# Moving the sum of phi(K) and the weight sums from GpSimd to VectorE, with relu on ScalarE and a fifth plain pair, in a two-layer linear-attention kernel

## The chip, the cores and the metric

The kernel runs on one core of a Trainium2 chip. The metric is the device time of one execution in microseconds (us); lower is better. A time is given as the median of several executions with the lowest and highest beside it.

The engines are written as the profile writes them: PE is the matmul engine, PEld its weight loads (they overlap PE), DVE is VectorE, ACT is ScalarE, POOL is GpSimd, SP is the engine whose queue issues DMAs. In the views `ps` is PSUM, which the matmuls write, and `arena` is the kernel's SBUF. L757 is line 757 of the kernel's source. The change removes and adds lines, so the same place has slightly different numbers before and after: L606 before is L605 after, L757 is L756, L676 is L675, L610 and L619 are L609 and L618, L929 is L927, L1125 is L1126.

## The reference, cut to what matters

Two identical layers follow each other. Each has a linear attention and a gated feed-forward part. S is 2048 tokens, D is 1024, and there are 32 heads of 32.

```python
def _A_ref(x, wqkv, wo):                      # x is already layer-normalised
    qkv = (x @ wqkv).reshape(B, S, 3, H, Dh) ...
    phi = lambda t: jnp.where(t > 0, t + 1, jnp.exp(t)) + 1e-6
    pq, pk = phi(q), phi(k)
    kv  = jnp.einsum("bhsd,bhse->bhde", pk, v)
    z   = jnp.einsum("bhsd->bhd", pk)         # the sum of phi(K) over all tokens
    num = jnp.einsum("bhqd,bhde->bhqe", pq, kv)
    den = jnp.einsum("bhqd,bhd->bhq", pq, z)[..., None] + 1e-6
    ...                                       # (num / den) @ wo

x = x + _A_ref(_layernorm(x), A_wqkv, A_wo)
x = x + _B_ref(_layernorm(x), B_w_gate, B_w_up, B_w_down)
# ... and both lines once more: the second layer, with the same weights
```

Only the K and Q projections, phi, and z are touched by the change.

## The kernel before

The kernel projects K and Q first. For this document that stretch is called the K/Q stage; the stage that forms K^T V starts when it ends. Tokens are handled in tiles of 128, two tiles are a pair, and there are eight pairs.

A pair can be projected in two ways. A *plain* pair takes 64 matmuls of 128x512 (K and Q, two tiles, two column halves, eight contraction steps each). A *quad* is a Strassen–Winograd product with seven block products of four matmuls, 28 for K or Q of one pair, so 56 for both. A quad needs sums of blocks of the weights ("weight sums") and of the normalised x, which are fp16. In layer one the weight sums don't exist yet and layer norms have only begun, so the kernel starts with four plain pairs; the weight sums are formed meanwhile, kept in DRAM, and loaded in layer two, where every pair is a quad.

```python
    NHOLD = 2
    NPL1 = 8
    LNX = (3, 5, 6)
    RLB = (7, 4)
```

`NPL1 = 8` is eight tiles, that is four plain pairs. `RLB` names the PSUM banks whose quad outputs get the relu form of phi, in layer one only.

phi of a 128x512 block has two forms. Both begin with an exponential by ScalarE and a `min(e, 1) + 1e-6` by VectorE. Then either VectorE reads the product from PSUM once more (`scalar_tensor_tensor`), or ScalarE writes `relu` of it to SBUF and VectorE adds two SBUF tiles (`tensor_tensor`).

```python
        def e_min(ev, er):
            P.add("dve", lambda e: e.tensor_scalar(out=ev, in0=ev, scalar1=1.0, scalar2=PHI0, op0=ALU.min, op1=ALU.add), rd=er, wr=er)

        def phi_exp(bank):
            ev, er = e_next()
            P.add("act", lambda e: e.activation(ev, psb(bank), AF.Exp), prd=[bank], wr=er)
            return ev, er

        rl = {"on": False, "n": 0}

        def phi_relu(bank):
            r = rl["n"] % 4
            rl["n"] += 1
            rv, rr = vh(O_XN[r // 2] + r % 2 * 1024, 512), R(O_XN[r // 2] + r % 2 * 1024, 1024)
            P.add("act", lambda e: e.activation(rv, psb(bank), AF.Relu), prd=[bank], wr=rr)
            return rv, rr

        def phi_out(bank, ev, er, dst_ap, dst_rng, rl_=None):
            e_min(ev, er)
            if rl_:
                rv, rr = rl_
                tt(dst_ap, rv, ev, ALU.add, rr + er, dst_rng)
                return
            P.add("dve", lambda e: e.scalar_tensor_tensor(out=dst_ap, in0=psb(bank), scalar=PHI1, in1=ev, op0=ALU.add, op1=ALU.max),
                  prd=[bank], rd=er, wr=dst_rng)

        def phi_evac(bank, dst_ap, dst_rng):
            ee = phi_exp(bank)
            phi_out(bank, *ee, dst_ap, dst_rng, phi_relu(bank) if rl["on"] else None)
```

The weight sums are subtractions of 128x2048 blocks, on whichever engine the caller names, cut into `parts` instructions:

```python
        def tw_make(n, eng, parts):
            b11, b12, b21, b22 = [w_blk(n, kb, h) for kb in range(2) for h in range(2)]
            t1, t2, t3, t4 = [tw_blk(n, c) for c in (1, 2, 3, 4)]
            step = 4 // parts
            ops = []
            for o, a, b in ((t1, b12, b11), (t2, b22, t1), (t4, b21, t2), (t3, b22, b12)):
                for k in range(0, 4, step):
                    def one(o=o, a=a, b=b, k=k):
                        P.add(eng, lambda e: e.tensor_tensor(out=o[0][:, k:k + step], in0=a[0][:, k:k + step], in1=b[0][:, k:k + step], op=ALU.subtract),
                              rd=rsub(a[1], k, step) + rsub(b[1], k, step), wr=rsub(o[1], k, step))
                    ops.append(one)
            return ops
```

Every finished half block of phi(K) is added on GpSimd to an fp32 accumulator; this is the sum over tokens:

```python
            def dst_of(kind, i, h):
                if kind == "k":
                    return pk[:, h, i, :], r_pk(i, h)
                return x_res[:, i, h * 512:(h + 1) * 512], r_x(i, h * 512, (h + 1) * 512)

            def z_add(i, h):
                za, pa = zacc[:, h * 512:(h + 1) * 512], pk[:, h, i, :]
                rz_ = R(O_ZACC + h * 2048, 2048)
                if h not in z_on:
                    z_on.add(h)
                    P.add("pool", lambda e: e.tensor_copy(za, pa), rd=r_pk(i, h), wr=rz_)
                else:
                    P.add("pool", lambda e: e.tensor_tensor(out=za, in0=za, in1=pa, op=ALU.add),
                          rd=r_pk(i, h) + rz_, wr=rz_)

            def proj(kind, i, h):
                t, v, c0, base = WSRC[kind]
                bank = B_KQ[kq_i[0] % len(B_KQ)]
                kq_i[0] += 1

                def fn(e):
                    return [e.matmul(psb(bank), xnT[:, k, i * 128:(i + 1) * 128], t[:, k, h * 512:(h + 1) * 512],
                                     start=(k == 0), stop=(k == KT - 1)) for k in range(KT)]
                P.add("pe", fn, rd=r_xT(i * 128, (i + 1) * 128) + r_w(base, h * 512, (h + 1) * 512), pwr=[bank])

                def ev():
                    phi_evac(bank, *dst_of(kind, i, h))
                    if kind == "k":
                        z_add(i, h)
                return ev
```

The quad gives four phi outputs, two of them through ScalarE's copy `u` and VectorE's `t1`; the two direct ones may use relu:

```python
                def ex(self, bank):
                    self.e = getattr(self, "e", {})
                    self.e[bank] = phi_exp(bank) + ((phi_relu(bank),) if rl["on"] and bank in RLB else (None,))

                def out(self, bank, i, h):
                    ev, er, r = self.e[bank]
                    phi_out(bank, ev, er, *dst_of(self.kind, i, h), r)
                    if self.kind == "k":
                        z_add(i, h)
        # ... cut ...
                def t1(self, j):
                    u, ru = self.u2 if j == 2 else self.u3
                    k = j - 2
                    P.add("dve", lambda e: e.scalar_tensor_tensor(out=t1sb[k], in0=psb(self.Y), scalar=PHI1, in1=u, op0=ALU.add, op1=ALU.add),
                          prd=[self.Y], rd=ru, wr=R(O_T1[k], 1024))
        # ... cut ...
                def out1(self, j, i, h):
                    k = j - 2
                    ev, er = self.e1[j]
                    d, rd_ = dst_of(self.kind, i, h)
                    e_min(ev, er)
                    tt(d, t1sb[k], ev, ALU.max, R(O_T1[k], 1024) + er, rd_)
                    if self.kind == "k":
                        z_add(i, h)
```

The plain part of layer one. The weight sums for K are four VectorE instructions, those for Q sixteen GpSimd instructions:

```python
            NPL = NPL1 if first else 0
            rl["on"] = first
            twk = []
            if first:
                twk = tw_make("k", "dve", 1)
                twq = tw_make("q", "pool", 4)
            seq = [("k", i) for i in range(NHOLD)] if NPL else []
            for i in range(NHOLD, NPL):
                seq += [("q", i - NHOLD), ("k", i)]
            seq += [("q", i) for i in range(max(NPL - NHOLD, 0), NPL if NPL < NST else 0)]
            npack = [0]
            for kind, i in seq:
                for h in range(2):
                    ev = proj(kind, tok[i], h)
                    ev()
                    if kind == "k":
                        lnstep(i, h)
                    elif twq and i >= 1:
                        for _ in range(2):
                            if len(twq) > 4:
                                twq.pop(0)()
                if kind == "q" and i >= 1 and len(twk) > 1:
                    twk.pop(0)()
```

At the end the accumulator is cast by ScalarE and reduced over partitions by a matmul with ones:

```python
            def z_final():
                for h in range(2):
                    P.add("pe", (lambda h: lambda e: e.matmul(psb(B_Z[h]), ones, zab[:, h * 512:(h + 1) * 512], start=True, stop=True))(h),
                          rd=R(O_ONES, 256) + R(O_A[1] + h * 1024, 1024), pwr=[B_Z[h]])
                    P.add("dve", (lambda h: lambda e: e.tensor_copy(zb[:, h * 512:(h + 1) * 512], psb(B_Z[h])))(h),
                          prd=[B_Z[h]], wr=R(O_ZB + h * 1024, 1024))
        # ... cut ...
            P.add("act", lambda e: e.copy(zab, zacc), rd=R(O_ZACC, D * 4), wr=R(O_A[1], D * 2))
```

## Time and profile before

The time before is 1489.12 us, the median of 3 runs (1489.07 to 1490.49). The profiled execution has a span of 1487.0 us.

The first fence is the page of the kernel before: busy time of each engine with its share of the span and its instructions, then the chain of work that ended last, by engine.

```profile
PE 1451.5 (98%) x7512; PEld 720.7 (48%) x7574; DVE 1182.1 (79%) x2218; ACT 595.3 (40%) x1201; POOL 234.0 (16%) x256
...
PE 69%; DVE 18%; DMA 7%; issue 3%; SPq 1%; ACT 1%; POOL 1%; DVEq 0%; ACTq 0%
...
```

PE is busy for 98% of the span, but in the chain DVE has 18%. A chain is followed back from the last instruction to whatever released each step, so for these 18% the end of the kernel hung on VectorE. It doesn't say in which stage; the next view does.

The table by stretches gives the busy time and instruction count of each engine in the K/Q stage of layer one (36 to 125 us) and of layer two (771 to 866 us). Columns after the window are its length, then busy us of PE, PEld, DVE, ACT and POOL, the granted clock, the DMA share and GB/s.

```profile
core 0: us, PE busy (x) PEld busy (x) DVE busy (x) ACT busy (x) POOL busy (x), PEclk, DMA share, GB/s
...
36.00:60.00 24.00, 22.52 (x108) 10.22 (x109) 23.41 (x37) 12.48 (x23) 21.71 (x21) 1.00 0.12 23
60.00:76.00 16.00, 11.42 (x52) 5.02 (x52) 15.41 (x35) 9.94 (x19) 11.02 (x13) 1.00 0.75 150
76.00:125.00 49.00, 43.88 (x183) 19.09 (x187) 47.01 (x92) 28.70 (x51) 24.60 (x24) 0.90 0.65 168
771.00:866.00 95.00, 88.56 (x391) 37.03 (x396) 92.02 (x184) 56.86 (x98) 38.94 (x38) 1.00 0.39 112
```

VectorE is busy for 23.41 of 24.00 us, 15.41 of 16.00, and 92.02 of 95.00. PE has gaps in every one of these windows. GpSimd is nearly full in the first (21.71 of 24.00), and after the switch to quads the granted clock is only 0.90.

The list of waits of PE between 60 and 125 us (engine and line, what it waited for, total us, times, longest):

```profile
engine line waited for: us in total, times, longest us
PE ps L907 <- DVE arena L757: 6.5, 1, 6.5
PE ps L907 <- DVE arena L676: 2.4, 1, 2.4
...
```

The timeline of PE over the same switch (start, length, what ran, and in brackets the idle time before it with its releaser):

```profile
...
71.00 1.03 PE L907 MATMUL ps<-arena 128*128 128x512 bf16 x4
78.52 4.81 PE L907 MATMUL ps<-arena 128*128 128x512 f16 x12 [6.49 <-DVE arena L757]
85.77 38.97 PE L907 MATMUL ps<-arena 128*128 128x512 f16 x169 [2.44 <-DVE arena L676]
124.58 1.67 PE L1125 MATMUL ps<-arena 128*128 128x512 bf16 x7
```

PE waits 6.49 us for a VectorE sum and 2.44 us for the last weight sum. After the first of these, twelve matmuls take 4.81 us, 0.40 us each; later in the stage they are spaced 0.216 us. So the waits cost more than their own 8.9 us: half clock comes on top. The Trainium skill, page "TensorE: Matmul & The Clock Gate", section "What's actually happening", states that the clock halves after at least one idle window of about 3.4 us and recovers after a busy one. The trace agrees for the first wait: the granted clock is 0.50 until 82.70 us. It also fell after the second, shorter wait: it is 0.50 again from 86.11 to 89.53 us.

In layer two there is no such long wait. PE's list of waits from 763.5 us to the end of the stage has many short ones, 5.9 us in all, most of them for VectorE (L929 is `t1`, L628 is the last step of phi from PSUM):

```profile
...
PE ps L907 <- DVE arena L929: 2.3, 5, 0.6
PE ps L907 <- DVE arena L757: 1.8, 2, 1.1
PE ps L907 <- ACT arena L914: 1.3, 7, 0.2
PE ps L907 <- DVE arena L628: 0.5, 2, 0.2
```

Why is VectorE slow there? The timeline of all engines in the plain part shows the same VectorE instruction alone and beside a GpSimd instruction.

```profile
...
38.69 0.29 DVE L606 TENSOR_SCALAR arena<-arena 128x512 bf16<-128x512 bf16 x1
39.01 0.43 DVE L757 TENSOR_TENSOR arena<-arena 128x512 bf16<-128x512 f16 x1
...
39.83 1.28 POOL L869 TENSOR_TENSOR arena<-arena 128x512 f32<-128x512 f32 x1
40.01 1.25 DVE L606 TENSOR_SCALAR arena<-arena 128x512 bf16<-128x512 bf16 x1
...
41.07 4.59 POOL L676 TENSOR_TENSOR arena<-arena 128x512 f16<-128x512 bf16 x3
...
41.30 1.26 DVE L757 TENSOR_TENSOR arena<-arena 128x512 bf16<-128x512 f16 x1
...
42.48 2.17 DVE L676 TENSOR_TENSOR arena<-arena 128x2048 f16<-128x2048 bf16 x1
...
```

Alone, the min (L606) takes 0.29 us and the 128x512 sum (L757) 0.43 us. Beside a GpSimd sum of 1.28 us the min takes 1.25 us. Beside GpSimd weight sums the sum takes 1.26 us, and VectorE's own weight sum of 2048 takes 2.17 us. The min ends at 41.26 us, 0.15 us after the GpSimd sum (41.11): that is what waiting looks like, not even slowing.

The Trainium skill, page "SBUF — State Buffer", section "Who interferes with whom", says that VectorE and GpSimd share one port pair under an exclusive lock, that "the other **fully blocks** (not throttle)", that a VectorE instruction with two SBUF inputs contends with a GpSimd instruction that reads SBUF but not with one that only writes it, and that `tensor_scalar` in its two-port modes contends with both. The min and the sum above agree with blocking; the experiments below test the distinction between reading and writing.

Checkpoints of the kernel before, read from PE's timeline:

| | us |
|---|---|
| layer one: first quad matmul | 71.0 |
| layer one: K^T V starts | 124.6 |
| layer two: first quad matmul | 763.5 |
| layer two: K^T V starts | 861.9 |
| span | 1487.0 |

### The profile page before, as it was taken

What the parts mean: (1) busy time and instruction counts of PE and PEld (TensorE: products, weight loads), DVE (VectorE), ACT (ScalarE), POOL (GpSimd) and SP (SyncE); (2) the same over time, 40 slices, a digit from 0 to 9 for tenths busy, and PEclk for the clock granted to TensorE, in tenths of its full rate; (3) what the DMA queues carried; (4) which work ended last, traced back from release to release, by engine and by line L of the source; (5) the groups of instructions that cost most, each with busy time, mean ns of one, the idle gap of its engine ahead of it and who ended that gap; (6) DMA issues with size and microseconds to landing.
All of it is one profiled execution on the core that took longest, in us unless ns stands there. A gap on an engine that the chain in (4) does not pass through costs nothing.

```text
span 1487.0 us, 20482 instructions
## 1 busy us (share of the span) xinstructions
PE 1451.5 (98%) x7512; PEld 720.7 (48%) x7574; DVE 1182.1 (79%) x2218; ACT 595.3 (40%) x1201; POOL 234.0 (16%) x256
## 2 busy tenths in 40 slices
PE   8889999999999999999998999999999999999999
PEld 3334444443444455554443444446666445666544
DVE  6998977867766599986569988789888675888853
ACT  5554247333310144451025633476666004666400
POOL 5853631000000000000013347210000000000000
PEclk9989999999999999999999999999999999999999
DMA  7386967999995667867485057676665756666642
GB/s 255 69 215 178 211 139 168 257 278 294 316 328 184 224 205 258 277 226 277 172 254 139 19 167 155 174 174 227 236 240 197 237 194 220 234 241 225 209 174 97
DMA packets 270163, 310.16 MB, mean 209 GB/s; under 512 B 161904, under 2 KB 212848, under 8 KB 270064
## 3 DMA queue, kind: packets, MB, share of 16 engines
q1 hardware_dynamic: 270064, 308.86, 67.9%
q8 instruction: 60, 0.98, 0.3%
q14 instruction: 39, 0.32, 0.1%
HBM read 230.16 MB, written 69.73 MB: 202 GB/s over the span
## 4 chain that ended last, share of the span: by engine, by line
PE 69%; DVE 18%; DMA 7%; issue 3%; SPq 1%; ACT 1%; POOL 1%; DVEq 0%; ACTq 0%
PE ps L1566 22%; PE ps L1307 21%; PE ps L1380 10%; PE ps L1125 7%; DVE arena L757 6%; DMA arena<-in_B_w_down_dram 5%; PE ps L1228 3%; PE ps L907 3%; DVE arena L606 3%; DVE arena L445 3%; DVE arena L760 2%; PE ps L878 2%; DMA arena<-arena 1%; DVE arena L929 1%; DVE arena L628 1%
## 5 line engine op out<-in xcount | busy, mean ns | idle before, releaser
L1307 PE MATMUL ps<-arena 128*128 128x512 f16 x2240 | 532.1, 379 | 3.5 <-ACT arena L1312 1.0
L757 DVE TENSOR_TENSOR arena<-arena 128x256 f32<-128x256 f32 (+6 forms) x999 | 465.8, 495 | 81.1 <-ACT arena L1384 31.6
L760 DVE SCALAR_TENSOR_TENSOR arena<-ps,arena 128x512 f16<-128x512 f32 (+2 forms) x564 | 372.3, 685 | 165.1 <-PE ps L1566 143.5
L1566 PE MATMUL ps<-arena 128*128 128x512 f16 (+1 forms) x1548 | 338.0, 379 | 1.1
L1307 PEld LDWEIGHTS ps<-arena 128*128 128x128 f16 (+1 forms) x2240 | 212.6, 98 | 219.1 <-ACT arena L1312 15.5
L1566 PEld LDWEIGHTS ps<-arena 128*128 128x128 f16 x1568 | 153.5, 98 | 183.9
L1380 PE MATMUL ps<-arena 128*128 128x256 f16 x1568 | 218.9, 273 | 2.4 <-ACT arena L1384 1.9
L1380 PEld LDWEIGHTS ps<-arena 128*128 128x128 f16 (+1 forms) x1568 | 149.1, 98 | 87.4 <-ACT arena L1384 13.6
L1384 ACT ACTIVATE arena<-ps 128x256 f32<-128x256 f32 x448 | 153.5, 383 | 76.7 <-PE ps L1380 73.1
L1333 ACT COPY ps<-ps 128x512 f32<-128x512 f32 x112 | 63.9, 570 | 289.7 <-PE ps L1307 288.6
L1312 ACT ACTIVATE arena<-ps 128x512 f32<-128x512 f32 x224 | 133.7, 597 | 103.6 <-PE ps L1307 91.8
L907 PE MATMUL ps<-arena 128*128 128x512 f16 (+1 forms) x606 | 140.9, 387 | 15.5 <-DVE arena L757 8.3
L1125 PE MATMUL ps<-arena 128*128 128x512 bf16 x498 | 114.7, 379 | 0.7
L448 POOL TENSOR_SCALAR arena<-arena 128x1 f32<-128x1 f32 x64 | 18.5, 290 | 604.8 <-DVE arena L447 604.5
L1228 PE MATMUL ps<-arena 128*128 128x512 bf16 x502 | 110.5, 379 | 1.8 <-ACT ps L1222 1.3
L907 PEld LDWEIGHTS ps<-arena 128*128 128x128 f16 x616 | 59.1, 99 | 96.5 <-issue 10.6
L445 DVE BATCH_NORM_STATS2 arena<-arena 128x6 f32<-128x512 bf16 x128 | 88.2, 689 | 10.6 <-DMA arena<-in_A_x_dram 6.3
L1011 POOL TENSOR_TENSOR arena<-arena 128x1024 f16<-128x1024 f32 x32 | 78.2, 2444 | 84.7 <-DVE arena L1009 74.7
L869 POOL TENSOR_TENSOR arena<-arena 128x512 f32<-128x512 f32 x60 | 71.9, 1200 | 77.3 <-DVE arena L757 45.5
L1228 PEld LDWEIGHTS ps<-arena 128*128 128x128 f16 x512 | 50.0, 98 | 62.0 <-ACT ps L1222 2.1
L878 PE MATMUL ps<-arena 128*128 128x512 bf16 x312 | 72.2, 385 | 4.9 <-DMA arena<-arena 1.9
L1125 PEld LDWEIGHTS ps<-arena 128*128 128x128 f16 x512 | 49.2, 98 | 55.7
(57 smaller groups left out, 731.8 us busy)
## 6 DMA issues: line engine op xcount, KB each, us to landing
arena<-w_scratch SPq DMA_DIRECT2D x84, 896.0 KB, 6.1
arena<-t_scratch SPq DMA_DIRECT2D x32, 896.0 KB, 5.8
arena<-in_B_w_down_dram SPq DMA_DIRECT2D x24, 896.0 KB, 6.7
w_scratch<-arena SPq DMA_DIRECT2D x28, 512.0 KB, 7.2
arena<-sp_scratch SPq DMA_DIRECT2D x28, 512.0 KB, 3.6
arena<-w_scratch SPq DMA_DIRECT2D x28, 384.0 KB, 5.6
x_scratch<-arena SPq DMA_DIRECT2D x36, 256.0 KB, 7.4
arena<-x_scratch SPq DMA_DIRECT2D x36, 256.0 KB, 6.1
```

The lines of the kernel that those rows point to most:

```text
L445: P.add("dve", (lambda h: lambda e: e.bn_stats(st[j][:, 6 * h:6 * h + 6], x_res[:, i, (D // 2) * h:(D // 2) * (h + 1)]))(h), rd=r_x(i, (D ...
L757: P.add("dve", lambda e: e.tensor_tensor(out=out, in0=a, in1=b, op=op), rd=rd, wr=wr, prd=prd)
L760: P.add("dve", lambda e: e.scalar_tensor_tensor(out=out, in0=a, scalar=sc, in1=b, op0=ALU.mult, op1=op1), rd=rd, wr=wr, prd=prd)
L878: return [e.matmul(psb(bank), xnT[:, k, i * 128:(i + 1) * 128], t[:, k, h * 512:(h + 1) * 512], start=(k == 0), stop=(k == KT - 1)) for k ...
L907: P.add("pe", lambda e: [e.matmul(psb(bank), a[0][:, k, :], b[0][:, k, :], start=(q in (1, 5) and k == 0), stop=(k == 3), skip_group_check ...
L1125: return [e.matmul(psb(bank), xrt[t][:, jj * 128:(jj + 1) * 128], pk[:, h, t, :], start=(t == tok[0]), stop=(t == tok[NST - 1])) for t in ts]
L1228: return [e.matmul(psb(bank), xnT[:, g, i * 128:(i + 1) * 128], wp[:, g, dh * 512:(dh + 1) * 512], start=(dh == 0 and g == 0), stop=(g == ...
L1307: P.add("pe", lambda e: [e.matmul(psb(bank), w[:, k, :], x[:, k, :], start=(start and k == 0), stop=(k == 3), skip_group_check=True) for k ...
L1312: P.add("act", lambda e: e.activation(t, psb(bank), AF.Copy, scale=SG), prd=[bank], wr=r)
L1380: P.add("pe", lambda e: [e.matmul(psb(bank)[:, 256 * half:256 * half + 256], w[:, k, :], xx[:, k, :], start=(start and k == 0), stop=(k == ...
L1384: P.add("act", lambda e: e.activation(dst, psb(bank)[:, 0:256], AF.Copy, scale=SG), prd=[bank], wr=rd_)
L1566: return [e.matmul(psb(bank), hv[:, 7 * hf + k, t * 128:(t + 1) * 128], w[:, k, :], start=(start and hf == 0 and k == 0), stop=(hf == 1 an ...
```

## The change

The intent is to leave GpSimd idle where VectorE binds, and to make up for the work that VectorE takes over:

- The sum of phi(K) becomes fp16 sums on VectorE, one or two per pair of tiles (14 instructions of 128x1024 per layer in place of 32 of 128x512 on GpSimd). There are two fp16 accumulators, which the final matmul with ones adds up in PSUM, so ScalarE's cast goes.
- The weight sums for Q become four VectorE instructions; the last of them is issued inside the first quad.
- relu by ScalarE is used for both direct outputs of every quad, in both layers.
- Layer one has five plain pairs instead of four.

```diff
--- before.py
+++ after.py
@@ -191,9 +191,9 @@
     PHI1 = 1.0 + 1e-6
     PE_WARM = 10
     NHOLD = 2
-    NPL1 = 8
+    NPL1 = 10
     LNX = (3, 5, 6)
-    RLB = (7, 4)
+    RLB = [(4, 5, 6, 7), (4, 5, 6, 7)]
     NPE_T = 6
     NNORM = 14
     YACT = True
@@ -364,8 +364,7 @@
         den = vf(O_DEN, 32)
         rden = vf(O_RDEN, 32)
         rz = vf(O_RZ, 8)
-        zacc = vf(O_ZACC, D)
-        zab = vb(O_A[1], D)
+        zacc = vh(O_ZACC, 2 * D).rearrange("p (a h c) -> p a h c", a=2, h=2)
         zb = vb(O_ZB, D)
         kvT = vb(O_KVT, D).rearrange("p (g c) -> p g c", c=128)
         GT = [vb(O_GT + i * 1024, 512) for i in range(4)]
@@ -613,9 +612,9 @@
         rl = {"on": False, "n": 0}
 
         def phi_relu(bank):
-            r = rl["n"] % 4
+            o = rl["o"] + rl["n"] % 2 * 1024
             rl["n"] += 1
-            rv, rr = vh(O_XN[r // 2] + r % 2 * 1024, 512), R(O_XN[r // 2] + r % 2 * 1024, 1024)
+            rv, rr = vh(o, 512), R(o, 1024)
             P.add("act", lambda e: e.activation(rv, psb(bank), AF.Relu), prd=[bank], wr=rr)
             return rv, rr
 
@@ -852,22 +851,23 @@
             kq_i = [0]
             tok = lnp.order
             QX, QZ, QY = [5, 6], [7, 4], [0, 1, 2]
-            z_on = set()
 
             def dst_of(kind, i, h):
                 if kind == "k":
                     return pk[:, h, i, :], r_pk(i, h)
                 return x_res[:, i, h * 512:(h + 1) * 512], r_x(i, h * 512, (h + 1) * 512)
 
-            def z_add(i, h):
-                za, pa = zacc[:, h * 512:(h + 1) * 512], pk[:, h, i, :]
-                rz_ = R(O_ZACC + h * 2048, 2048)
-                if h not in z_on:
-                    z_on.add(h)
-                    P.add("pool", lambda e: e.tensor_copy(za, pa), rd=r_pk(i, h), wr=rz_)
+            def z_pair(p):
+                i, i2, c = tok[2 * p], tok[2 * p + 1], p // 4
+                za, rz_ = zacc[:, c], R(O_ZACC + c * 2048, 2048)
+                o = O_XN[1] if first or p >= 4 else O_XRT[tok[NST - 1]]
+                zt, rt = vh(o, D).rearrange("p (h c) -> p h c", c=512), R(o, D * 2)
+                rp = [r for j in (i, i2) for h in range(2) for r in r_pk(j, h)]
+                if p % 4 == 0:
+                    tt(za, pk[:, :, i, :], pk[:, :, i2, :], ALU.add, rp, rz_)
                 else:
-                    P.add("pool", lambda e: e.tensor_tensor(out=za, in0=za, in1=pa, op=ALU.add),
-                          rd=r_pk(i, h) + rz_, wr=rz_)
+                    tt(zt, pk[:, :, i, :], pk[:, :, i2, :], ALU.add, rp, rt)
+                    tt(za, za, zt, ALU.add, rz_ + rt, rz_)
 
             def proj(kind, i, h):
                 t, v, c0, base = WSRC[kind]
@@ -881,8 +881,8 @@
 
                 def ev():
                     phi_evac(bank, *dst_of(kind, i, h))
-                    if kind == "k":
-                        z_add(i, h)
+                    if kind == "k" and tok.index(i) % 2 and h:
+                        z_pair(tok.index(i) // 2)
                 return ev
 
             class Quad:
@@ -915,13 +915,11 @@
 
                 def ex(self, bank):
                     self.e = getattr(self, "e", {})
-                    self.e[bank] = phi_exp(bank) + ((phi_relu(bank),) if rl["on"] and bank in RLB else (None,))
+                    self.e[bank] = phi_exp(bank) + ((phi_relu(bank),) if bank in RLB[not first] else (None,))
 
                 def out(self, bank, i, h):
                     ev, er, r = self.e[bank]
                     phi_out(bank, ev, er, *dst_of(self.kind, i, h), r)
-                    if self.kind == "k":
-                        z_add(i, h)
 
                 def t1(self, j):
                     u, ru = self.u2 if j == 2 else self.u3
@@ -942,8 +940,8 @@
                     d, rd_ = dst_of(self.kind, i, h)
                     e_min(ev, er)
                     tt(d, t1sb[k], ev, ALU.max, R(O_T1[k], 1024) + er, rd_)
-                    if self.kind == "k":
-                        z_add(i, h)
+                    if self.kind == "k" and j == 2:
+                        z_pair(self.p)
 
             def quads(items, hook, fill):
                 b = c = None
@@ -1033,11 +1031,11 @@
             else:
                 lnp.use_dma = True
             NPL = NPL1 if first else 0
-            rl["on"] = first
+            rl.update(on=first, o=O_XN[0] if first else O_XRT[tok[NST - 2]])
             twk = []
             if first:
                 twk = tw_make("k", "dve", 1)
-                twq = tw_make("q", "pool", 4)
+                twq = tw_make("q", "dve", 1)
             seq = [("k", i) for i in range(NHOLD)] if NPL else []
             for i in range(NHOLD, NPL):
                 seq += [("q", i - NHOLD), ("k", i)]
@@ -1049,12 +1047,10 @@
                     ev()
                     if kind == "k":
                         lnstep(i, h)
-                    elif twq and i >= 1:
-                        for _ in range(2):
-                            if len(twq) > 4:
-                                twq.pop(0)()
                 if kind == "q" and i >= 1 and len(twk) > 1:
                     twk.pop(0)()
+                elif kind == "q" and i >= 1 and len(twq) > 1:
+                    twq.pop(0)()
                 if kind == "q" and NPL < NST and i in LNX:
                     for h in range(2):
                         lnstep(NPE_T, h)
@@ -1071,16 +1067,19 @@
                 items += [("k", p), ("q", p)]
             if npr < 8:
                 items += [("k", 6), ("k", 7), ("q", 6)]
-            if first:
-                for f in twk + twq:
-                    f()
-                for w in "kq":
-                    for c in (1, 2, 4, 3):
-                        tw_store(w, c)
             jobs = {}
 
             def job(n, j, f):
                 jobs.setdefault((n, j), []).append(f)
+            if first:
+                for f in twk:
+                    f()
+                for f in twq[:-1]:
+                    f()
+                for w, c in (("k", 1), ("k", 2), ("k", 4), ("k", 3), ("q", 1), ("q", 2), ("q", 4)):
+                    tw_store(w, c)
+                job(0, 2, twq[-1])
+                job(0, 3, lambda: tw_store("q", 3))
             for n, (kind, p) in enumerate(items):
                 if kind == "k" and n:
                     sm = s_make(tok, p)
@@ -1101,6 +1100,8 @@
                     if (n + 1) * c // m > n * c // m:
                         job(n, 3, pack)
                 elif n >= 1:
+                    if n == 9:
+                        job(n, 0, lambda: rl.update(o=O_XN[0]))
                     job(n, 0, lnp.flush_b)
                     job(n, 2, lnp.flush_a)
 
@@ -1160,8 +1161,8 @@
 
             def z_final():
                 for h in range(2):
-                    P.add("pe", (lambda h: lambda e: e.matmul(psb(B_Z[h]), ones, zab[:, h * 512:(h + 1) * 512], start=True, stop=True))(h),
-                          rd=R(O_ONES, 256) + R(O_A[1] + h * 1024, 1024), pwr=[B_Z[h]])
+                    P.add("pe", (lambda h: lambda e: [e.matmul(psb(B_Z[h]), ones, zacc[:, a, h], start=(a == 0), stop=(a == 1)) for a in range(2)])(h),
+                          rd=R(O_ONES, 256) + R(O_ZACC, 4096), pwr=[B_Z[h]])
                     P.add("dve", (lambda h: lambda e: e.tensor_copy(zb[:, h * 512:(h + 1) * 512], psb(B_Z[h])))(h),
                           prd=[B_Z[h]], wr=R(O_ZB + h * 1024, 1024))
 
@@ -1172,7 +1173,6 @@
                 P.add("dve", lambda e: e.reciprocal(rz, psb(B_Z[0])[:, 0:NG]), prd=[B_Z[0]], wr=R(O_RZ, 32))
 
             na = [0]
-            P.add("act", lambda e: e.copy(zab, zacc), rd=R(O_ZACC, D * 4), wr=R(O_A[1], D * 2))
 
             def wprod(n, bank, on_act):
                 dh, g = n // NG, n % NG
```

## The prediction

> **What bounds the kernel now.** The page has PE busy 98% of the 1487.0 us span. The change touches the two K/Q stages, where VectorE binds (table by stretches):
> - Layer one, 36 to 60 and 60 to 76 us: VectorE busy 23.4 of 24 and 15.4 of 16 us. At the switch from plain to Strassen products PE stands 6.5 us (until 78.5) for an f16 sum of VectorE, then 2.4 us for the last weight sum (list of waits); matmuls then start every 0.425 us instead of 0.216 until about 89.6 (timeline; granted clock 0.90 in 76 to 125).
> - Layer two, 771 to 866 us: VectorE 92.0 of 95 us. Two quads take 15.7 us up to about 811, while layer norms run, then 12.3, against 12.1 of matmuls (56 x 0.2157). From 763.5 to 867.3 there are 436 matmuls, 94 us: 9.7 us are lost.
>
> VectorE is slow there because of GpSimd: in the timeline its 128x512 min takes 0.28 us alone, 1.25 when a GpSimd sum (1.2 us, 60 of them) or weight sum (1.4 us, 16) runs; sums of 0.43 us become 1.26, the 2048-wide weight sum 2.17 instead of 1.21. The Trainium skill, "SBUF — State Buffer", "Who interferes with whom", says that both share a port pair under an exclusive lock; the trace agrees.
>
> **Removed, added, moved.**
> - All sums, copies and weight sums leave GpSimd. VectorE gets 14 pair sums of 1024 f16 per layer, estimated 0.6 to 0.7 us each (between 0.43 at 512 and 1.21 at 2048), about 9 us, and in layer one 4 weight sums, 1.2 each. Against that I estimate 30 us of blocked VectorE time gone in layer one and 0.85 us per quad in the layer-norm part of layer two.
> - Relu by ScalarE: the VectorE step from PSUM (start to start 0.61 us) becomes an f16 sum (0.34): 0.27 us less for 30 outputs in layer two, 5 in layer one. ScalarE gets 0.49 us each, 15 us in layer two where it was busy 57 of 95: it fits.
> - A fifth plain pair: 64 instead of 56 matmuls, +1.7 us of PE, but more time for layer norms and weight sums before the quads.
> - The 1.03 us cast of the sums goes; off the path.
>
> **On the critical path.** Layer one: the plain part (40 projections, 69 us, plus cold start, transposes, 3.5 us of gaps) should end near 85 us with VectorE nearly caught up; a stall of 0 to 3 us; then five quads at full clock, 30 us. The K-V stage, now starting at 124.6 us, starts near 115: 9 us saved (5 to 13). Layer two: two quads of the layer-norm part need 14.1 us of VectorE instead of 15.7; with smaller gaps at both ends 6 us saved (2 to 9). Later stages are PE-bound (over 99% from 120 to 240 us); in the first gate/up stage DMA is at 97%, but PE stands only 2 us, so the gain should be kept.
>
> **Prediction: 1474 us, 1465 to 1483 in 8 of 10.** Faster by over 2%: 0.03; within 2%: 0.96; slower: 0.01.
>
> **What would show it.** Right: no GpSimd sums in the K/Q stages; VectorE min at 0.28 us everywhere; full clock from 76 to 125; K-V stage near 115 us; layer two's first quads at about 14 us a pair. Wrong: PE still waiting for VectorE at the switch (VectorE needs an estimated 93% of PE's time in the plain part).
>
> **What would make it wrong.** Two relu buffers instead of four couple ScalarE to VectorE and hold PSUM banks; pair sums come in lumps; ScalarE's longer queue delays copies that PE waits for; DMA in layer one gives the time back.

## The result, and the profile after

The kernel after took 1471.15 us (median of 4, 1470.52 to 1472.75), the kernel before in the same rounds 1489.09 us (median of 4, 1488.46 to 1490.49). The ratio is 0.988 with a 95% interval of 0.9863 to 0.9897. Ratios here are the mean time of one kernel's runs over that of the other's of the same rounds, so they are not quite the ratio of the medians quoted. The outputs are correct.

| checkpoint | before, us | after, us | difference |
|---|---|---|---|
| layer one: first quad matmul | 71.00 | 83.35 | (a fifth plain pair) |
| layer one: K^T V starts | 124.58 | 113.41 | -11.2 |
| layer two: first quad matmul | 763.50 | 751.80 | -11.7 |
| layer two: K^T V starts | 861.85 | 843.80 | -18.05 |
| span | 1487.0 | 1469.6 | -17.4 |

So layer one gives 11.2 us, the K/Q stage of layer two gives another 6.35 (98.35 us long before, 92.00 after), and what lies between and after them neither adds nor takes more than 0.7 us.

The page of the kernel after, the same lines:

```profile
PE 1451.0 (99%) x7586; PEld 722.1 (49%) x7586; DVE 1149.7 (78%) x2242; ACT 607.5 (41%) x1234; POOL 137.8 (9%) x176
...
PE 73%; DVE 13%; DMA 8%; issue 3%; ACT 2%; POOL 1%; SPq 1%; DVEq 0%; ACTq 0%
...
```

PE does the same busy time in a shorter span. VectorE's share of the chain fell from 18% to 13% and GpSimd's instructions from 256 to 176.

The table by stretches of the kernel after, with the same columns; the layer-two window has moved with the stage:

```profile
...
36.00:60.00 24.00, 24.00 (x119) 11.14 (x118) 21.65 (x48) 15.76 (x28) 5.49 (x9) 1.00 0.38 77
60.00:76.00 16.00, 16.00 (x76) 7.26 (x75) 15.42 (x34) 8.58 (x16) 4.83 (x8) 1.00 0.48 91
76.00:125.00 49.00, 47.77 (x223) 21.16 (x221) 39.28 (x97) 32.78 (x60) 2.65 (x4) 1.00 0.80 231
752.00:844.00 92.00, 89.75 (x413) 39.69 (x412) 81.73 (x203) 70.81 (x129) 5.06 (x12) 1.00 0.42 126
```

In the plain part PE is now busy for all of 24.00 and all of 16.00 us. GpSimd's time falls from 21.71 to 5.49 and from 11.02 to 4.83 us; what is left are tiny instructions of the layer norms. VectorE is still close to full there (21.65 and 15.42), although it has taken work over. From 76 to 125 us the clock is 1.00. In layer two VectorE has 10 us to spare, and ScalarE went from 56.86 to 70.81 us, 14 us more, close to the 15 us that relu was to cost it.

The list of waits of PE in the same stretch, and its timeline at the switch:

```profile
...
PE ps L907 <- ACT arena L609: 0.7, 1, 0.7
PE ps L907 <- DVE arena L756: 0.3, 1, 0.3
...
```

```profile
...
83.35 1.03 PE L907 MATMUL ps<-arena 128*128 128x512 bf16 x4
84.70 3.00 PE L907 MATMUL ps<-arena 128*128 128x512 f16 x12 [0.33 <-DVE arena L756]
88.38 25.20 PE L907 MATMUL ps<-arena 128*128 128x512 f16 x116 [0.68 <-ACT arena L609]
113.41 1.89 PE L1126 MATMUL ps<-arena 128*128 128x512 bf16 x8
...
```

The waits of 6.5 and 2.4 us are 0.3 and 0.7 us, and the quads take 30.06 us (83.35 to 113.41) for 132 matmuls. At 0.2157 us each, the spacing of the last 116 of them, that is 28.5 us of matmuls and 1.6 us lost. Before it was 53.58 us for 188 matmuls: 40.55 us and 13.0 lost.

In the K/Q stage of layer two the list of PE's waits has shrunk from 5.9 to 2.2 us:

```profile
...
PE ps L907 <- ACT arena L914: 1.2, 3, 0.5
PE ps L907 <- DVE arena L927: 1.0, 1, 1.0
```

The timeline of all engines, in the plain part of the kernel after:

```profile
...
60.42 0.29 DVE L605 TENSOR_SCALAR arena<-arena 128x512 bf16<-128x512 bf16 x1
...
60.74 0.42 DVE L756 TENSOR_TENSOR arena<-arena 128x512 bf16<-128x512 f16 x1
...
61.75 1.22 DVE L675 TENSOR_TENSOR arena<-arena 128x2048 f16<-128x2048 bf16 x1
...
```

The min takes 0.29 us, the sum 0.42, the weight sum 1.22. For the first two these are the times that they had alone before. 1.22 us for a sum of two bf16 inputs of 2048 elements is also what the Trainium skill gives for a `tensor_tensor` of that length with bf16 operands in SBUF (1224 ns; page "VectorE: DVE Perf Modes", section "The perf-mode tier table (the rule you actually need)"), so it can be taken for VectorE's undisturbed time, as the prediction did with the 1.21 us it read from the trace.

### The profile page after: what moved, and what is told of

Its sections match the earlier page's. It is cut to its first block, busy times and chain, and to the rows that moved or that the text cites. A ratio compares the mean times of both kernels' runs of the same rounds, so it can differ in the third digit from the quotient of the medians.

```text
span 1469.6 us, 20519 instructions
## 1 busy us (share of the span) xinstructions
PE 1451.0 (99%) x7586; PEld 722.1 (49%) x7586; DVE 1149.7 (78%) x2242; ACT 607.5 (41%) x1234; POOL 137.8 (9%) x176
## 4 chain that ended last, share of the span: by engine, by line
PE 73%; DVE 13%; DMA 8%; issue 3%; ACT 2%; POOL 1%; SPq 1%; DVEq 0%; ACTq 0%
PE ps L1566 23%; PE ps L1307 21%; PE ps L1380 10%; PE ps L1126 8%; PE ps L907 6%; DMA arena<-in_B_w_down_dram 5%; DVE arena L756 4%; PE ps L878 3%; DVE arena L444 3%; DVE arena L759 2%; DMA arena<-arena 2%; DMA arena<-w_scratch 1%; PE ps L1228 1%; SPq L417 1%; DMA arena<-in_A_wqkv_dram 1%
## 5 line engine op out<-in xcount | busy, mean ns | idle before, releaser
L756 DVE TENSOR_TENSOR arena<-arena 128x512 f16<-128x512 f16 (+8 forms) x1060 | 485.9, 488 | 84.7 <-ACT arena L1384 31.9
L1566 PE MATMUL ps<-arena 128*128 128x512 f16 (+1 forms) x1568 | 339.7, 379 | 0.0
L1566 PEld LDWEIGHTS ps<-arena 128*128 128x128 f16 x1568 | 153.3, 98 | 184.0
L907 PE MATMUL ps<-arena 128*128 128x512 f16 (+1 forms) x560 | 123.2, 379 | 3.3 <-ACT arena L914 1.2
L1126 PE MATMUL ps<-arena 128*128 128x512 bf16 x512 | 116.1, 379 | 0.0
L1228 PE MATMUL ps<-arena 128*128 128x512 bf16 x512 | 111.0, 379 | 1.3 <-ACT ps L1222 1.3
L878 PE MATMUL ps<-arena 128*128 128x512 bf16 x384 | 86.9, 383 | 3.2 <-ACT arena L548 1.6
L907 PEld LDWEIGHTS ps<-arena 128*128 128x128 f16 x560 | 53.9, 98 | 71.6 <-ACT arena L914 5.4
L1228 PEld LDWEIGHTS ps<-arena 128*128 128x128 f16 x512 | 50.0, 98 | 62.0 <-ACT ps L1222 2.3
L1126 PEld LDWEIGHTS ps<-arena 128*128 128x128 f16 x512 | 49.3, 98 | 55.7
L609 ACT ACTIVATE arena<-ps 128x512 bf16<-128x512 f32 x88 | 53.0, 602 | 39.8 <-PE ps L878 27.8
```

Of the source, the lines that this page charges most:

```text
L756: P.add("dve", lambda e: e.tensor_tensor(out=out, in0=a, in1=b, op=op), rd=rd, wr=wr, prd=prd)
L907: P.add("pe", lambda e: [e.matmul(psb(bank), a[0][:, k, :], b[0][:, k, :], start=(q in (1, 5) and k == 0), stop=(k == 3), skip_group_check ...
L1126: return [e.matmul(psb(bank), xrt[t][:, jj * 128:(jj + 1) * 128], pk[:, h, t, :], start=(t == tok[0]), stop=(t == tok[NST - 1])) for t in ts]
L1228: return [e.matmul(psb(bank), xnT[:, g, i * 128:(i + 1) * 128], wp[:, g, dh * 512:(dh + 1) * 512], start=(dh == 0 and g == 0), stop=(g == ...
L1566: return [e.matmul(psb(bank), hv[:, 7 * hf + k, t * 128:(t + 1) * 128], w[:, k, :], start=(start and hf == 0 and k == 0), stop=(hf == 1 an ...
```

## The experiments

The theory: **nearly all of the gain comes from GpSimd no longer blocking VectorE**; relu and the plain pair are small additions that use the freed time. The rivals:

- *Time at the switch*: the 9 us wait at the switch is closed by the fifth plain pair, which gives VectorE 14 us more before the quads.
- *Dependencies*: it is the waiting for GpSimd's results (weight sums, sums of phi(K)) that cost, not the sharing.
- *ScalarE*: the saving is the cheaper last step of phi.

Each kernel below is the kernel after with one thing edited, unless it says otherwise, and all ran correctly. They ran in three groups, each on one chip with its own runs of the kernel before (7 in each group; medians 1489.34, 1488.15 and 1489.40). "Loss" is how much of the gain a kernel gave up: its median minus that of before, against the -17.9 us of the kernel after.

| run | median us | before of same rounds | ratio, 95% interval | loss, us |
|---|---|---|---|---|
| pairs_on_gpsimd | 1488.21 | 1489.34 | 0.9993, 0.9978 to 1.0007 | 16.8 |
| wsums_on_gpsimd | 1482.65 | 1489.34 | 0.9957, 0.9940 to 0.9973 | 11.2 |
| relu_as_before | 1474.81 | 1489.34 | 0.9903, 0.9888 to 0.9918 | 3.4 |
| four_plain | 1476.19 | 1489.34 | 0.9912, 0.9897 to 0.9927 | 4.8 |
| sums_only | 1477.33 | 1488.15 | 0.9925, 0.9907 to 0.9944 | 7.1 |
| before_five_plain | 1486.10 | 1488.15 | 0.9982, 0.9962 to 1.0002 | 15.9 |
| dummy_reads | 1497.24 | 1488.15 | 1.0060, 1.0037 to 1.0084 | 27.0 |
| dummy_writes | 1475.25 | 1488.15 | 0.9912, 0.9894 to 0.9931 | 5.0 |
| after_again | 1472.49 | 1489.40 | 0.9881, 0.9862 to 0.9901 | 1.0 |
| six_plain | 1476.20 | 1489.40 | 0.9909, 0.9892 to 0.9927 | 4.7 |
| relu_z_layer_two | 1473.49 | 1489.40 | 0.9893, 0.9876 to 0.9911 | 2.0 |
| relu_x_layer_two | 1473.65 | 1489.40 | 0.9890, 0.9873 to 0.9907 | 2.2 |

The kernel after, run again, differs by 1.0 us from its first result: differences of that size are not resolved.

### 1. The pair sums back on GpSimd

```diff
 def z_pair(p):
-    tt(za, pk[:, :, i, :], pk[:, :, i2, :], ALU.add, rp, rz_)          # and the two other sums
+    ptt(za, pk[:, :, i, :], pk[:, :, i2, :], rp, rz_)                  # the same sum, P.add("pool", ...)
```

> The kernel after, with only the engine of the pair sums changed from VectorE to GpSimd (same arithmetic, same buffers, 14 sums of 1024 f16 per layer). Theory 'lock' (VectorE was slow because GpSimd held a shared port): VectorE is spared 9 us per layer but blocked for about 2 us at each of the 28 GpSimd sums; mins of VectorE of over 1 us come back (they last 0.29 us in the kernel after) and the time rises by 6 to 14 us, to about 1477 to 1485. Rival 'schedule and relu' (the fifth plain pair and the relu did it, the engine of the sums matters little): within 3 us of 1471, as VectorE has less work.

It took 1488.21 us: almost the whole gain is gone, more than the 14 us expected at most. The K^T V stages start at 120.8 us (after: 113.4) and 859.4 us; the layer-two stage is 100.66 us long instead of 92.00. VectorE has *less* work here than in the kernel after. The timeline of this kernel in layer two shows why that doesn't help:

```profile
...
788.54 4.39 POOL L861 TENSOR_TENSOR arena<-arena 128x1024 f16<-128x1024 bf16 x2 [2.55 <-DVE arena L756]
...
788.70 4.51 DVE L756 TENSOR_TENSOR arena<-arena 128x512 bf16<-128x512 f16 x2
...
797.32 1.04 PE L910 MATMUL ps<-arena 128*128 128x512 bf16 x4 [3.34 <-DVE arena L930]
...
```

Two VectorE sums that take 0.42 us each alone end up as one entry of 4.51 us, beside two GpSimd sums that take 4.39 us. PE, a few us later, waits 3.34 us for VectorE's `t1` (L930 in this kernel). Fourteen sums per layer, whose results no VectorE instruction uses, cost almost what the whole change gained.

### 2. The weight sums for Q back on GpSimd

```diff
-                twq = tw_make("q", "dve", 1)
+                twp = tw_make("q", "pool", 4)
+                twq = [(lambda k=k: [f() for f in twp[4 * k:4 * k + 4]]) for k in range(4)]
```

> The kernel after, with only the four q weight sums put back on GpSimd in 16 pieces. Theory 'lock': VectorE is spared 4.9 us but blocked by 16 pieces of 1.4 us in the plain part of layer one; PE waits again at the switch; the time rises by 3 to 8 us, all before 115 us; layer two as in the kernel after. Rival 'schedule and relu': no change (under 2 us).

It took 1482.65 us, a loss of 11.2 us, above the range of 3 to 8. K^T V of layer one starts at 122.4 us, 9.0 later than after. The layer-two stage, which forms no weight sums, is exactly as long as in the kernel after, 92.00 us, which was the control. A further 2.8 us are lost between the two; the list of waits has 2.5 us there for VectorE in the first gate and up stage. This run mixes blocking with waiting for the results of GpSimd, so it does not by itself separate the theory from the rival of dependencies.

### 3. relu as before

```diff
-    RLB = [(4, 5, 6, 7), (4, 5, 6, 7)]
+    RLB = [(7, 4), ()]
```

> The kernel after, with relu by ScalarE only where the kernel before had it (layer one, all plain outputs and two of the four quad banks; none in layer two). Theory 'lock': VectorE gets 0.27 us more for 30 outputs of layer two, of which only those in the layer-norm part (about 12 outputs) are on the path: 2 to 4 us slower, 1473 to 1475. Rival 'relu' (freeing PSUM banks early by ScalarE did most of it): 8 us or more slower.

It took 1474.81 us, a loss of 3.4 us, within the 2 to 4 expected. The layer-two stage is 94.75 us long, 2.75 more than after. relu is a real but small part, and the rival *ScalarE* falls as the main cause.

### 4. Four plain pairs

```diff
-    NPL1 = 10
+    NPL1 = 8
```

> The kernel after, with four plain pairs in layer one as before. Theory 'lock': PE has 1.7 us less of matmuls, VectorE has less time for layer norms and weight sums before the quads and waits cost about as much or somewhat more: between 1 us faster and 4 us slower. Rival 'schedule' (the fifth pair did most of layer one's gain): 8 us or more slower, with the 6 us wait at the switch back.

It took 1476.19 us, a loss of 4.8 us, just outside the range of the theory (-1 to 4) and short of the 8 that *time at the switch* demanded. The timeline of PE at the switch of this kernel:

```profile
...
68.55 1.03 PE L907 MATMUL ps<-arena 128*128 128x512 bf16 x4
73.91 42.17 PE L907 MATMUL ps<-arena 128*128 128x512 f16 x184 [4.33 <-DVE arena L756]
115.91 1.89 PE L1126 MATMUL ps<-arena 128*128 128x512 bf16 x8
...
```

With an undisturbed VectorE and four plain pairs, the wait at the switch is 4.33 us instead of the 8.9 us of the kernel before. It is still long enough for the clock to fall: the ten matmuls from 73.91 us on take 4.45 us, about 2.3 us more than at full clock. So the fifth pair does real work that the theory undervalued: it takes the rest of the wait away, and with it the drop of the clock. At the switch that explains 2.5 us (K^T V of layer one starts at 115.91 instead of 113.41 us). At the first quad of layer two the kernel is 4.1 us behind; where the further 1.6 us arise is not shown. The price of such a wait also varies: in run 5 below, a wait of 4.30 us at the same place was followed by 3.41 us at half clock, here by 6.83.

### 5. The sums alone

```diff
-    NPL1 = 10
+    NPL1 = 8
-    RLB = [(4, 5, 6, 7), (4, 5, 6, 7)]
+    RLB = [(7, 4), ()]
```

> The kernel after with four plain pairs and relu as before: of the change only the moves from GpSimd to VectorE (pair sums in f16, weight sums) are left. If the parts add up as the single undoings did (relu 3.7 us, fifth pair 5.0 us), 1479 to 1481 us; theory 'lock' holds if it keeps 8 us or more of the 18 us by itself with VectorE doing more work than in the kernel before. A rival in which the parts help only together: within 3 us of 1489.

It took 1477.33 us, 10.8 us faster than before, better than the 1479 to 1481 expected. Moving the sums (with their new form and order, and the cast gone) is 10.8 of 17.9 us, without the fifth plain pair and without relu in more places. relu and the fifth pair together add the other 7.1, slightly less than their two separate losses (3.4 and 4.8).

### 6. The fifth plain pair alone, in the kernel before

```diff
 # in the kernel before
-    NPL1 = 8
+    NPL1 = 10
```

> The kernel before with a fifth plain pair alone; GpSimd keeps all its sums. Theory 'lock': VectorE stays 13 us behind PE at the switch whatever the number of plain pairs, PE has 1.7 us more to do: between 2 us slower and 3 us faster than before. Rival 'schedule': 4 us faster or more, as undoing the fifth pair in the kernel after cost 5 us.

It took 1486.10 us, 2.05 less than before by the medians. The interval of the ratio, 0.9962 to 1.0002, reaches from 5.7 us faster to 0.3 us slower, so the times alone do not quite exclude the 4 us that the rival needed. The timeline of PE in this kernel:

```profile
...
84.35 1.03 PE L907 MATMUL ps<-arena 128*128 128x512 bf16 x4
91.02 4.25 PE L907 MATMUL ps<-arena 128*128 128x512 f16 x12 [5.64 <-DVE arena L757]
96.48 25.20 PE L907 MATMUL ps<-arena 128*128 128x512 f16 x116 [1.21 <-ACT arena L619]
121.52 1.89 PE L1125 MATMUL ps<-arena 128*128 128x512 bf16 x8
...
```

The switch comes 13 us later, and PE still waits 5.64 us and then another 1.21; the twelve matmuls between them take 4.25 us, most of them at half clock. More time before the switch is of little use as long as VectorE, blocked by GpSimd, also falls behind in that time. *Time at the switch* falls as the main cause: run 5 has 10.8 of the 17.9 us without the pair, and here most of the wait stays with it. It is worth 4.8 us after VectorE is freed.

### 7. Useless sums on GpSimd

After each of the K outputs (32 half blocks per layer), two GpSimd sums read 352 columns of it as both inputs and write to a scratch tile that nothing reads. VectorE keeps all the work of the kernel after.

```diff
+            def dum(rr, pd):
+                for _ in range(2):
+                    P.add("pool", lambda e: e.tensor_tensor(out=vb(O_DUM, 352), in0=pd, in1=pd, op=ALU.add), rd=rr, wr=R(O_DUM, 704))
...
+                    if self.kind == "k":
+                        dum(r_pk(i, h), pk[:, h, i, 0:352])
```

> The kernel after plus two useless GpSimd sums (352 bf16 elements read from the new phi(K), written to 704 spare bytes that nobody reads) after each of the 64 half blocks of phi(K); no instruction waits for them. Theory 'lock': VectorE mins and sums that meet them last 0.8 us or more and the time rises by 6 to 16 us, though nothing depends on the sums. Rival 'waits' (the gain came from VectorE, PE or DMA no longer waiting for results of GpSimd): under 1 us slower.

It took 1497.24 us, 27 us of loss and slower than the kernel before; 6 to 16 were expected. The trace lists no instruction that waits for these sums. GpSimd's own layer-norm instructions queue behind them, but VectorE's listed waits for GpSimd add up to 11.5 us in this run and 10.0 in the kernel after, so *dependencies* explain at most a small part of it. The groups of instructions by shape tell where it went. First the kernel after, 751 to 845 us (engine, operation, shapes and count, then busy us and mean ns of one, then idle time before):

```profile
...
L756 DVE TENSOR_TENSOR arena<-arena 128x512 bf16<-128x512 f16 x56 | 23.8, 425 | 3.1 <-ACT arena L618 1.3
...
L605 DVE TENSOR_SCALAR arena<-arena 128x512 bf16<-128x512 bf16 x56 | 16.0, 286 | 5.8 <-ACT arena L933 3.1 <-ACT arena L609 2.7
...
```

Then this kernel, 751 to 865 us (L758 and L607 are the same sum and min):

```profile
...
L864 POOL TENSOR_TENSOR arena<-arena 128x352 bf16<-128x352 bf16 x54 | 47.8, 885 | 40.3 <-DVE arena L758 38.2
...
L758 DVE TENSOR_TENSOR arena<-arena 128x512 bf16<-128x512 f16 x52 | 31.4, 603 | 2.3 <-ACT arena L620 0.5
L607 DVE TENSOR_SCALAR arena<-arena 128x512 bf16<-128x512 bf16 x52 | 24.1, 464 | 2.2 <-ACT arena L611 2.2
...
```

The sum went from 425 to 603 ns and the min from 286 to 464. The instructions are the same; only GpSimd's 885 ns reads stand beside them. For the two groups that is 52 times 0.178 us twice, 18.5 us of VectorE time, and the stage grew from 92.00 to 105.53 us.

### 8. Useless writes on GpSimd

The same places and about the same GpSimd time, but four `memset`s that read nothing:

```diff
-                for _ in range(2):
-                    P.add("pool", lambda e: e.tensor_tensor(out=vb(O_DUM, 352), in0=pd, in1=pd, op=ALU.add), rd=rr, wr=R(O_DUM, 704))
+                for _ in range(4):
+                    P.add("pool", lambda e: e.memset(vb(O_DUM, 352), 0.0), rd=rr, wr=R(O_DUM, 704))
```

> As the run with useless sums, but four GpSimd memsets of 352 bf16 in their place: GpSimd only writes. If VectorE and GpSimd share a read and a write port as the Trainium skill says (SBUF - State Buffer, Who interferes with whom), two-input sums of VectorE stay at 0.42 us, while one-input mins, if they run in a two-port mode, still meet the memsets and lengthen: 0 to 6 us slower, less than half of what the sums cost. If only reading collides: no change in either.

It took 1475.25 us, a loss of 5.0 us, within 0 to 6. The groups of this kernel in the same window:

```profile
...
L864 POOL MEMSET arena<- 128x352 bf16 x128 | 51.3, 401 | 35.7 <-DVE arena L758 28.8
...
L758 DVE TENSOR_TENSOR arena<-arena 128x512 bf16<-128x512 f16 x60 | 25.5, 425 | 3.2 <-ACT arena L620 1.3
L607 DVE TENSOR_SCALAR arena<-arena 128x512 bf16<-128x512 bf16 x60 | 22.8, 381 | 5.4 <-ACT arena L611 3.0 <-ACT arena L943 2.0
...
```

GpSimd is busy for 51.3 us, no less than in the run before, but the sum with two SBUF inputs keeps its 425 ns. Only the `tensor_scalar` instructions grow: the min from 286 to 381, the one of the layer norm (128x1024) from 539 to 569. This is the distinction that the skill's "Who interferes with whom" makes, and the trace agrees with both halves of it. The two runs together show the mechanism: what costs VectorE the time is chiefly GpSimd's reading of SBUF, not its being busy and not its results. Writes alone still cost something, through the min; in this run's profile 3.41 us at half clock (791.66 to 795.07 us) are part of it.

### 9. The kernel after, again

> The kernel after, unchanged, as the yardstick on the chip of the next three: 1470 to 1473 us.

No edit. 1472.49 us, as expected; the checkpoints are 112.7, 753.1 and 845.1 us. It is the base of the next three, which ran on the same chip.

### 10. Six plain pairs

```diff
-    NPL1 = 10
+    NPL1 = 12
```

> The kernel after with a sixth plain pair. PE has 1.7 us more of matmuls; with five pairs PE waited only about 1 us at the switch, so there is little left to win: 1 to 2 us slower than the kernel after. A rival that more plain pairs are simply better: faster by 1 us or more.

It took 1476.20 us, 3.7 more than the kernel after on the same chip; 1 to 2 were expected, from the eight extra matmuls (1.7 us). At K^T V of layer one it is only 0.5 us behind (113.16 against 112.67 us). The other part comes later: PE waits 1.8 us for a VectorE sum in the first gate and up stage, and by the start of layer two the delay is 2.2 us. At K^T V of layer two the delay is still 2.2 us, and the profiled span is 4.4 us longer in the end (1474.8 against 1470.4), so the rest arises after the K/Q stages. What causes it stays open. Five pairs is the best of four, five and six.

### 11 and 12. relu for half of the outputs in layer two

The prediction named ScalarE's longer queue as a danger. X and Z are the PSUM banks of a quad's two direct outputs (X: 5 and 6, Z: 7 and 4). These two kernels give relu in layer two only to the Z outputs, or only to the X outputs.

```diff
-    RLB = [(4, 5, 6, 7), (4, 5, 6, 7)]
+    RLB = [(4, 5, 6, 7), (7, 4)]       # relu_z_layer_two
+    RLB = [(4, 5, 6, 7), (5, 6)]       # relu_x_layer_two
```

> The kernel after with relu by ScalarE in layer two only for the two Z banks (15 of 30 outputs), the X banks by VectorE from PSUM. If ScalarE's longer queue in layer two (copies that PE waits for, 0.51 us at a time) costs as much as it spares VectorE: equal or up to 1.5 us faster than the kernel after. If VectorE's time alone counts: 1 to 2 us slower, half of what undoing relu cost.

> The kernel after with relu by ScalarE in layer two only for the two X banks. Relu on X stands just ahead of the copy of X that PE waits for, so it should be the worse half to keep: 1 to 3 us slower than the kernel after, and slower than the run with Z alone. If only VectorE's time counts, the same as with Z alone.

They took 1473.49 and 1473.65 us, about 1 us more than the kernel after of the same rounds, with overlapping ranges (after: 1470.80 to 1472.74; these: 1472.81 to 1475.61 and 1471.67 to 1474.48). In layer two PE waits less for ScalarE and more for VectorE: 1.2 us for ScalarE's copy and 1.0 for VectorE's `t1` in the kernel after. With relu for Z alone it is 0.6 for the copy, 0.2 for `t1` and 2.0 for phi's last step from PSUM (L627); with X alone 0.7 for the copy and 2.1 for `t1`. The balance of the kernel after is not improved by moving half back, so no experiment beats it.

## Why the prediction was right

The prediction was 1474 us with 1465 to 1483, within 2%; measured 1471.15, ratio 0.988. Point by point:

- **What binds.** VectorE in both K/Q stages, slowed by GpSimd. Shown: with everything on VectorE (sums_only) the time falls by 10.8 us although VectorE gets more instructions; with useless GpSimd reads added, 27 us come back.
- **Layer one: 9 us saved (5 to 13).** Measured 11.2. The sum of it: the plain part ends 12.35 us later for 64 more matmuls, which are 13.8 us, so its own gaps shrank by 1.45; the waits and the half clock after the switch shrank from 13.0 to 1.6 us, 11.4 less; eight more matmuls cost 1.7. That is -1.45 - 11.4 + 1.7 = -11.2. The term that was mis-sized is the end of the plain part and what follows: predicted near 85 us with a stall of 0 to 3, then 30 of quads, together about 115; measured 83.35, then 30.06 with all stalls included, 113.41. The prediction kept all 3.5 us of gaps that the plain part had before; about 1.5 us of them went.
- **Blocked VectorE time in layer one: about 30 us.** From the mean durations in both traces between 5 and 115 us: 48 mins at 527 instead of 286 ns are 11.6 us, 44 sums of phi at 574 instead of 425 ns 6.6, four weight sums at 1.93 instead of 1.22 us 2.9, and fifteen fp16 sums at 515 instead of 419 ns 1.4: 22 us. The estimate was a third too high. It had no effect on the predicted time because the prediction only needed VectorE to keep up with PE, and with 21.65 of 24.00 and 15.42 of 16.00 us busy it just does. That is 92.7% of the 40 us, and the prediction had put VectorE's need in the plain part at 93% of PE's time.
- **Layer two: 6 us saved (2 to 9).** Measured 6.35. The two quads of the layer-norm part were to take 14.1 us of VectorE instead of 15.7: from the starts of the layer-norm statistics on VectorE, they take 13.7 and 14.5 instead of 15.73. The blocked time here, from the means between 763 and 870 us before: 59 mins at 497 instead of 286 ns are 12.4 us and 29 fp16 sums at 465 instead of 415 ns 1.5, against some 8.3 us of pair sums added. Of the 6.35 us, the stage of run 5 (94.72 us long) has 3.6 from the sums, and relu brings the other 2.7. Pair sums were estimated at 0.6 to 0.7 us; they take 692 ns.
- **The gain is kept.** The later stages of layer one start 10.8 to 11.9 us earlier at each checkpoint, and layer two starts 11.7 us earlier.
- **relu fits ScalarE.** Its busy time in the stage rose from 56.86 to 70.81 us, and PE waits 1.2 us for it. The dangers named (two buffers, the longer queue, pair sums in lumps) cost no more than the 2.2 us of waits left in that stage, and giving ScalarE less relu didn't help.
- **"VectorE min at 0.28 us everywhere"** holds in the K/Q stages (mean 286 ns). It does not hold for the whole kernel: one of its 128 mins still takes 1.185 us (the next longest 0.305), at 179.29 us beside GpSimd's normalisation of the attention output, which the change leaves in place.

The attribution that the runs support: about 11 of 18 us for taking the sums off GpSimd by itself, and about 7 for relu and the fifth plain pair together, which come on top once that is done. So the theory holds in its mechanism, but "nearly all" was too strong: the two additions are two fifths of the gain. Of those, the fifth pair alone brought about 2 us to the kernel before, not resolved from nothing; relu alone in the kernel before was not run. The losses of the four undoings (16.8, 11.2, 3.4 and 4.8) add up to 36, twice the gain. They are not shares. Each undoing hits the same nearly full VectorE, and a delay that makes PE stand for long enough also halves its clock. A part of the cause that only one undoing shows must therefore not be read as what that part gained.

## What to carry to other kernels

When VectorE binds a stage, judge work on GpSimd by the VectorE time that it blocks, not by being off the path: compare the mean duration of one VectorE operation in that stage with its shortest. Look first at GpSimd instructions that read SBUF; those that only wrote cost about a fifth here for the same GpSimd time. When a binding engine has been relieved, re-tune the split that was tuned around it: the fifth plain pair was worth nothing measurable before and 4.8 us after.

## What the Trainium skill lacked or had wrong

- "SBUF — State Buffer", "Who interferes with whom", has the rule and it held. For its size the page has two slow-downs (6.8 and 1.5 times) without the instructions that they were measured on. Here two VectorE sums of 0.42 us took 4.51 us beside two GpSimd sums of 4.39; 64 useless GpSimd sums per layer, 0.885 us each in layer two, cost the kernel 27 us in two layers; memsets of about the same GpSimd time cost 5.0.
- "Perfetto Trace Analysis", "Optimizing Scalar/DVE Operations", says that moving work between GpSimd and VectorE "might not help". That understates it: giving VectorE's 14 pair sums per layer to GpSimd cost 16.8 us, although VectorE was the fuller engine.
- "TensorE: Matmul & The Clock Gate", "What's actually happening", names an idle window of about 3.4 us but not how idle it must be. After waits of 6.49, 5.64 and 4.33 us the matmuls ran at half clock, as the page says. They also did after waits of 2.44 us (before), 3.34 (pairs_on_gpsimd), 2.11 (wsums_on_gpsimd) and 2.37 (dummy_reads). In the 3.4 us just before those four drops PE had been busy for 0.97, 1.04, 1.30 and 1.03 us. After a wait of 2.83 us in wsums_on_gpsimd (from 73.83 us) the clock stayed full, so the length of a wait alone does not decide it.
- Nothing else that was used here was found wrong.
